# First block of a fused retention and two-FFN kernel: x split in two halves of 256 tokens, the first halves of two d_ff tiles between the attention chunks, weight conversion three steps ahead

## Chip, cores and metric

One NeuronCore of a Trainium2 chip runs the whole program in one launch. The metric is the device time of one execution in microseconds. Before the change three runs gave 883.71, 883.96 and 885.22 us: median 883.96 us.

## What is computed

A retention (linear attention with decay, no softmax) feeds an FFN with leaky ReLU, and that feeds an FFN with h·cos(h):

```python
def _attn_ref(q, k, v):                    # 4 batches, 8 heads, 576 tokens, 64 wide
    scores = scale * np.matmul(q, k.transpose(0, 1, 3, 2))
    Dmat = np.where(rel >= 0, gamma[:, None, None] ** rel[None, :, :], 0.0)
    return np.matmul(scores * Dmat[None], v)
x = attn_out.transpose(0, 2, 1, 3).reshape(2304, 512)
h = x @ w_in                               # d_ff = 2048
x = np.maximum(0.01 * h, h) @ w_out        # first FFN
h = x @ w_in2
out = (h * np.cos(h)) @ w_out2             # second FFN
```

## The kernel before

**Blocks and steps.** The 2304 tokens are five blocks (`TB`: 512, 512, 512, 384, 384). Each FFN runs over all blocks; a block goes through the 16 tiles f of 128 of d_ff, and one tile is a step s. `h_mm` (line 385) makes h of the step: 12 matmuls (4 parts of d_model, 3 products each) into one PSUM bank. `o_mm` (line 402) multiplies the tile of two steps earlier (`LAG`) with w_out, again 12 matmuls. So a step has 24 matmuls with up to 512 columns.

**Three products.** Operands of the FFN matmuls are float32r in two parts, high and low. `h_mm` issues for each part of d_model high weight by low x, low weight by high x, high by high: its first matmul needs the tile's high weight and the low x, its second the low weight. The x of a block is split by `split_x` (line 373): per part of d_model one copy on ACT (line 380: the high part) and one subtraction on DVE (line 381: the low part). After the first layer g is split the same way by `g_high` (ACT, line 455) and `g_low` (DVE, line 460).

**Weight conversion.** The raw weights arrive as 64-bit words. Each tile of the first FFN (a grain: 15 whole tiles, the last in two halves) is converted in five parts: `ready` calls `conv_a` (ACT, lines 307 and 308), `conv_b` (DVE, lines 313, 315, 319; a function `between` may be called ahead of line 319), `add_of` calls `conv_c` (DVE, line 326), `high_of` calls `conv_d` (ACT, line 335: the high weight), `low_of` calls `conv_e` (DVE, line 338: the low weight). Two buffers hold the grains under way, so `ready` of a grain needs the low part of the one two earlier.

**Retention.** It goes in chunks of 128 tokens: scale q and v by tables (line 135 on DVE for the first chunks), `scores` (line 166), `masks` (DVE, line 182), `values` (lines 197 and 211), `states` (DVE, lines 229 and 231: the running state), `reads` (line 244: the state's part), `take` (ACT, line 270: scaled output from PSUM to `xr`). Chunks 0 to 3 are the first block's x and run ahead of the steps; chunk 4 starts with `scores` after step 3 of the first block and follows the scaling of its q on DVE.

**What sets the order.** Under `manual_schedule` each engine runs its instructions in the order in which the code emits them. In the part ahead of the steps (lines 572 to 636) the four chunks, the conversion of grains 0 and 1 and the split of x are written out by hand:

```python
        conv_b(grains[1], second)          # line 619; second() is states(2)
        reads(2); take(2); states(3); reads(3); take(3)
        ...
        add_of(1); split_x(0); high_of(1); low_of(1); ready(2)
```

In the steps of the first block (lines 656 to 673) `conv_b` and `add_of` work on grain s + 2, `ready` on s + 3, and `low_of` on s + 1. The 16 matmuls of zeros at line 585 (`warm`) run on PE while the first data arrive.

Of the kernel before, what the change touches and what calls it, by code (L numbers as in the profile page):

```python
# [7 lines left out]
F32 = mybir.dt.float32  # L8
# [11 lines left out]
P = 128  # L20
# [48 lines left out]
def retention_ffn_ffn(  # L69
# [29 lines left out]
        tabs_sb[:, sum(sizes[:x]) : sum(sizes[: x + 1])] for x in range(4)  # L99
    )  # L100

    zero = xp.tile([P, 2 * T], F32, tag="x", name="zero")[:, :P]
    one = const.tile([P, 1], F32, name="one")
    psum = psp.tile([P, 8, 512], F32, name="psum")

# [83 lines left out]
    def values(i):  # L189
        b, ch, pt = banks_of(i), ch_t[i], p_t.pop(i)  # L190
        local = [(2 * i + x) % SUBS for x in range(2)]
        for p in range(NP):
            for x, tok in enumerate(halves):
                for e, r in enumerate(halves):
                    h = slice((2 * p + e) * D, (2 * p + e + 1) * D)
                    o = NP * C + p * C
                    nc.tensor.matmul(  # L197
                        psum[r, b + x, o : o + C],
                        ch[tok, 3, h],
                        pt[tok, e, p, :],  # L200
                        start=p == 0,
                        stop=local[x] == 0,
                        skip_group_check=True,
                    )
        for p in range(NP):
            for x, tok in enumerate(halves):
                if local[x] == SUBS - 1:
                    continue
                for e, r in enumerate(halves):
                    h = slice((2 * p + e) * D, (2 * p + e + 1) * D)  # L210
                    nc.tensor.matmul(  # L211
                        psum[r, b + x, p * D : (p + 1) * D],
                        ch[tok, 2, h],
                        ch[tok, 3, h],
                        start=False,
                        stop=True,
                        skip_group_check=True,
                    )
# [56 lines left out]
                )  # L275


    def warm(n, bank):
        for _ in range(n):
            nc.tensor.matmul(psum[:, bank, :P], zero, zero, start=True, stop=True)  # L280

# [26 lines left out]
    def conv_b(g, between=lambda: None):  # L310
        lo, hi = words(g)
        t = t_t[g]
        nc.vector.tensor_scalar(t, t, W_LO, W_HI, op0=ALU.max, op1=ALU.min)  # L313
        u = t.bitcast(U32)
        nc.vector.tensor_scalar(  # L315
            u, u, 3, 0x3FFFFFF8, op0=ALU.logical_shift_left, op1=ALU.bitwise_and
        )
        between()
        nc.vector.scalar_tensor_tensor(  # L319
            out=u, in0=hi, scalar=0xC0000000, in1=u, op0=ALU.bitwise_and, op1=ALU.bitwise_or  # L320
        )
# [49 lines left out]
            x_t[lj, k] = x  # L371
            nc.sync.dma_start(x[:, :, :n].bitcast(F32), x2[lj - NB][k])

    def split_x(lj):
        n = TB[lj]
        for k in range(KK):
            x = xp.tile([P, 2, T], F32R, tag="x", name="x_sb")
            x_t[lj, k] = x
            raw = xr.pop((lj, k))[:, :n]
            nc.scalar.copy(x[:, 0, :n], raw)  # L380
            nc.vector.tensor_tensor(  # L381
                out=x[:, 1, :n], in0=raw, in1=x[:, 0, :n].bitcast(F32), op=ALU.subtract
            )

    def h_mm(lj, f):
        l, n = lj // NB, TB[lj % NB]
        bank = BANK_H + (f % 2 if l == 0 else f % 4)
        hp = psum[:, bank, :n]
        h_t[lj, f] = hp
        wt, hi = w_t[l, f], l  # L390
        for k in range(KK):
            ks = slice(k * P, (k + 1) * P)
            for a, (i, j) in enumerate(((0, 1), (1, 0), (0, 0))):
                nc.tensor.matmul(  # L394
                    hp,
                    wt[:, i ^ hi, ks],
                    x_t[lj, k][:, j, :n],
                    start=(k == 0 and a == 0),
                    stop=(k == KK - 1 and a == 2),
                )  # L400
# [171 lines left out]
    with tc.manual_schedule():  # L572
        nc.scalar.dma_start(tabs_sb, tabs)
        nc.vector.memset(zero, 0.0)

        nc.scalar.copy(one, zero[:, :1])
        load_chunk(0)
        load_raw(0)
        for i in range(1, n_first):
            load_chunk(i)  # L580
        for f in range(1, 4):
            load_raw(f)
        scale_q(0)
        scale_v(0)
        warm(WARM[0], 3)
        scores(0)
        masks(0)
        ready(0)
        values(0)
        scale_v(1)  # L590
        conv_b(grains[0], lambda: scale_q(1))
        scores(1)
        masks(1)
        values(1)
        scale_v(2)
        states(0)
        reads(0)
        take(0)
        scale_q(2)
        scores(2)  # L600
        add_of(0)
        high_of(0)
        scale_q(3)
        scores(3)
        masks(2)
        ready(1)
        scale_v(3)
        values(2)
        low_of(0)
        masks(3)  # L610
        states(1)
        reads(1)
        take(1)
        values(3)

        def second():
            states(2)

        conv_b(grains[1], second)
        reads(2)  # L620
        take(2)
        states(3)
        reads(3)
        take(3)
        load_chunk(4)
        load_raw(4)
        load_chunk(5)
        for f in range(5, 10):
            load_raw(f)
        for _ in range(2):  # L630
            next_half()
        add_of(1)
        split_x(0)
        high_of(1)
        low_of(1)
        ready(2)

        for s in range(len(steps) + LAG[1]):
            lj, f = steps[s] if s < len(steps) else (None, None)
            i = chunk_at.get(s)  # L640
            if lj is not None:
                nxt = lj + 1 if lj + 1 < 2 * NB else None
                if s == last:
                    early.close()
                    fp = ctx.enter_context(tc.tile_pool(name="fp", bufs=2))
                if f == 2 and nxt is not None and nxt >= NB:
                    load_x(nxt)
                h_mm(lj, f)
                if f == NF - 1 and nxt is not None and nxt < NB:
                    split_x(nxt)  # L650
                if i is not None:
                    values(i)
                if s + 1 in chunk_at:
                    scores(chunk_at[s + 1])
            prev = steps[s - 1] if 1 <= s <= len(steps) else None
            if lj is not None and lj < NB:
                leaky(lj, f)
                if s < NF:

                    def between():  # L660
                        if s:
                            low_of(s + 1)
                        if s in (1, 2):
                            g_low(*prev)

                    if s + 2 < len(grains):
                        conv_b(grains[s + 2], between)
                    else:
                        between()
                    add_of(s + 2)  # L670
                    ready(s + 3)
                    high_of(s + 2)
                g_high(lj, f)
            if i is not None:
                states(i)
            if s + 1 in chunk_at:
                masks(chunk_at[s + 1])
            if n_first <= chunk_at.get(s + 2, 0) < n_busy:
                scale_q(chunk_at[s + 2])
                scale_v(chunk_at[s + 2])  # L680
            if prev and prev[0] < NB and prev in graw:
                g_low(*prev)
            for q in outs.get(s, ()):
                o_mm(*q)
            if i is not None:
                reads(i)
                take(i)
                if i + 2 < NCH:
                    load_chunk(i + 2)
                    if i + 2 >= n_busy:  # L690
                        scale_q(i + 2)
                        scale_v(i + 2)
            for q in outs.get(s, ()):
                if q[1] == NF - 1:
                    if lj is not None and lj < NB:

                        g_low(lj, f)
                    evacuate(q[0])
            if lj is not None and lj >= NB:
                cos_a(lj, f)  # L700
            if prev and prev[0] >= NB:
                cos_c(*prev)
            if lj is not None and lj >= NB:
                cos_b(lj, f)
            if prev and prev[0] >= NB:
                g_low(*prev)
            stash(s)
            for qj, qf in outs.get(s - 1, ()):
                if qj == NB - 1:
                    fetch_w(qf)  # L710
# [49 lines left out]
```

## Time and profile before

| what | value |
|---|---|
| median of three runs | 883.96 us |
| the profiled execution, its own time | 884.21 us |
| its span, first to last instruction | 882.4 us |
| PE busy | 862.1 us (98% of the span) |
| DVE busy | 577.0 us (65%) |
| ACT busy | 397.9 us (45%) |
| mean granted TensorE clock | 0.988 |

The profiled execution is 0.25 us above the median, and 1.8 us of its time lie outside the span. PE is the matmul engine, PEld its weight loads, DVE VectorE, ACT ScalarE, POOL GpSimd, SP the queue that issues most DMAs. A busy PE is not PE at its peak: matmuls overlap, and at the granted clock 0.50 they take about twice as long. Idle time of an engine costs only where PE or the chain that ends last waits for it.

### The profile page before, as it was taken

The page shows a single profiled execution, that of the slowest core. Times are in us where ns is not written, and L with a number is a line of the kernel's source. Part 1 is how long each engine was busy: PE and PEld are TensorE (multiplying, and loading weights), DVE is VectorE, ACT ScalarE, POOL GpSimd, SP SyncE. Part 2 cuts the span into 40 slices and gives each one's busy share as a digit, 9 for nine tenths or more (in the row PEclk, how much of TensorE's full clock was granted, in tenths as well). Part 3 has the DMA queues.
Part 4 walks back from the last instruction along what each step waited for, and adds up shares of the span by engine and source line. Part 5 has one row for each costly group of instructions (what it writes and reads, how often), then busy time and mean ns, then how long its engine had stood idle before and what let it go on. Part 6 is the DMA issues. An engine that isn't in the chain of part 4 may idle for free.

```text
span 882.4 us, 14824 instructions
## 1 busy us (share of the span) xinstructions
PE 862.1 (98%) x6048; PEld 752.6 (85%) x6048; DVE 577.0 (65%) x953; ACT 397.9 (45%) x738; POOL 69.0 (8%) x57
## 2 busy tenths in 40 slices
PE   6689999999999999999999999999999999999998
PEld 6568888778888888999999888888888888999998
DVE  5699964344644346644212897777777777888885
ACT  4588764434454446444322443343334333433433
POOL 0000020222212222211000000000000000000000
PEclk8699999999999999999999999999999999999999
DMA  9915421545464546641787700210021002100100
GB/s 362 418 48 196 184 100 72 192 168 175 161 238 144 192 147 247 218 155 49 284 305 245 262 1 1 95 49 1 1 72 48 1 1 72 49 1 1 37 1 36
DMA packets 35860, 110.88 MB, mean 126 GB/s; under 512 B 3408, under 2 KB 8528, under 8 KB 31696
## 3 DMA queue, kind: packets, MB, share of 16 engines
q1 hardware_dynamic: 35648, 109.59, 34.1%
q8 instruction: 47, 0.77, 0.4%
q10 hardware_dynamic: 144, 0.35, 0.1%
q14 instruction: 21, 0.17, 0.1%
HBM read 79.00 MB, written 30.93 MB: 125 GB/s over the span
## 4 chain that ended last, share of the span: by engine, by line
PE 94%; DVE 2%; DMA 1%; issue 1%; ACT 1%; SPq 0%; ACTq 0%
PE psum L408 45%; PE psum L394 44%; PE psum L244 2%; PE psum L166 1%; PE psum L197 1%; DMA raw<-in_w 1%; PE psum L211 1%; DVE t L326 1%; DVE t L319 1%; DVE w L338 0%; ACT t L307 0%; DVE g L460 0%; DVE t L313 0%; DVE t L315 0%; DVE p_sb L182 0%
## 5 line engine op out<-in xcount | busy, mean ns | idle before, releaser
L394 PE MATMUL psum<-x_sb,w 128*128 128x512 f32 (+1 forms) x1920 | 424.9, 370 | 4.2 <-DVE x_sb L381 2.5
L408 PE MATMUL psum<-g,w 128*128 128x512 f32 (+1 forms) x1920 | 424.1, 369 | 0.0
L394 PEld LDWEIGHTS psum<-x_sb,w 128*128 128x128 f32 x1920 | 351.0, 189 | 51.5 <-DVE x_sb L381 2.7
L408 PEld LDWEIGHTS psum<-g,w 128*128 128x128 f32 x1920 | 347.9, 188 | 46.7 <-DVE g L460 0.4
L455 ACT CAST g<-graw 128x512 fp32r<-128x512 f32 (+1 forms) x160 | 92.7, 579 | 238.3 <-PE psum L408 126.1
L460 DVE TENSOR_TENSOR g<-graw,g 128x512 fp32r<-128x512 f32 (+1 forms) x160 | 103.0, 645 | 92.1 <-ACT g L455 92.0
L478 ACT ACTIVATE r_sb<-r_sb 128x512 f32<-128x512 f32 (+1 forms) x80 | 47.3, 591 | 131.6 <-DVE r_sb L477 131.4
L468 DVE TENSOR_SCALAR t_sb<-psum 128x512 f32<-128x512 f32 (+1 forms) x80 | 51.0, 637 | 62.9 <-PE psum L394 62.9
L446 ACT ACTIVATE graw<-psum 128x512 f32<-128x512 f32 (+1 forms) x80 | 44.2, 553 | 57.9 <-PE psum L394 57.6
L476 DVE SCALAR_TENSOR_TENSOR r_sb<-t_sb,r_sb 128x512 f32<-128x512 f32 (+1 forms) x80 | 51.2, 640 | 2.8
L477 DVE SCALAR_TENSOR_TENSOR r_sb<-t_sb,r_sb 128x512 f32<-128x512 f32 (+1 forms) x80 | 51.1, 639 | 2.7
L475 DVE SCALAR_TENSOR_TENSOR r_sb<-t_sb,psum 128x512 f32<-128x512 f32 (+1 forms) x80 | 50.8, 635 | 2.8
L350 POOL TENSOR_TENSOR t<-t 128x512 fp32r<-128x512 f32 x32 | 42.6, 1338 | 126.9 <-ACT t L349 105.8
L484 DVE SCALAR_TENSOR_TENSOR graw<-r_sb,psum 128x512 f32<-128x512 f32 (+1 forms) x80 | 50.0, 625 | 1.7 <-ACT r_sb L479 1.7
L479 ACT ACTIVATE r_sb<-r_sb 128x512 f32<-128x512 f32 (+1 forms) x80 | 47.2, 590 | 2.5
L307 ACT ACTIVATE t<-raw 128x512 f32<-128x512 f32 (+1 forms) x49 | 39.9, 815 | 11.9 <-DMA raw<-in_w 8.0
L326 DVE CUSTOM_DVE_ANT_0 t<-raw,t 128x1024 uint16<-128x1024 uint16 (+1 forms) x49 | 41.9, 856 | 4.8
L319 DVE SCALAR_TENSOR_TENSOR t<-raw,t 128x512 uint32<-128x512 uint32 (+1 forms) x49 | 43.6, 891 | 1.1
L313 DVE TENSOR_SCALAR t<-t 128x512 f32<-128x512 f32 (+1 forms) x49 | 28.8, 587 | 18.7 <-ACT t L307 18.5
L182 DVE TENSOR_TENSOR p_sb<-psum,tabs_sb 128x512 f32<-128x512 f32 x18 | 12.4, 689 | 42.5 <-PE psum L166 40.9
L308 ACT ACTIVATE raw<-raw 128x512 int32<-128x512 uint32 (+1 forms) x49 | 39.8, 812 | 0.0
L473 DVE TENSOR_SCALAR t_sb<-t_sb 128x512 f32<-128x512 f32 (+1 forms) x80 | 31.6, 394 | 0.0
(35 smaller groups left out, 351.7 us busy)
## 6 DMA issues: line engine op xcount, KB each, us to landing
ch<-in_qkv SPq DMA_DIRECT2D x17, 1024.0 KB, 5.3
raw<-in_w SPq DMA_DIRECT2D x34, 512.0 KB, 4.2
w<-t SPq DMA_DIRECT2D x32, 512.0 KB, 3.0
w<-w SPq DMA_DIRECT2D x32, 512.0 KB, 5.2
raw<-in_w SPq DMA_DIRECT2D x15, 1024.0 KB, 8.7
x_sb<-x SPq DMA_DIRECT2D x12, 512.0 KB, 6.2
x<-x_hi SPq DMA_DIRECT2D x12, 256.0 KB, 2.5
x<-x_lo SPq DMA_DIRECT2D x12, 256.0 KB, 2.7
```

The costliest lines, as they stand in the source:

```text
L319: nc.vector.scalar_tensor_tensor(out=u, in0=hi, scalar=0xC0000000, in1=u, op0=ALU.bitwise_and, op1=ALU.bitwise_or)
L326: nc.vector.tensor_tensor(out=i, in0=i, in1=lo.bitcast(I32), op=ALU.add)
L394: nc.tensor.matmul(hp, wt[:, i ^ hi, ks], x_t[lj, k][:, j, :n], start=(k == 0 and a == 0), stop=(k == KK - 1 and a == 2),)
L408: nc.tensor.matmul(psum[:, BANK_O + m, :n], wt[:, i ^ hi, ms], gt[:, j, :n], start=(f == 0 and a == 0), stop=(f == NF - 1 and a == 2),)
L455: nc.scalar.copy(g_t[lj, f][:, 0, : TB[lj % NB]], g)
L460: nc.vector.tensor_tensor(out=gt[:, 1, :n], in0=graw.pop((lj, f)), in1=gt[:, 0, :n].bitcast(F32), op=ALU.subtract)
L468: nc.vector.tensor_scalar(t, h_t[lj, f], INV_2PI, MAGIC, op0=ALU.mult, op1=ALU.add)
L475: nc.vector.scalar_tensor_tensor(out=r, in0=t, scalar=-C1, in1=hp, op0=ALU.mult, op1=ALU.add)
L476: nc.vector.scalar_tensor_tensor(out=r, in0=t, scalar=-C2, in1=r, op0=ALU.mult, op1=ALU.add)
L477: nc.vector.scalar_tensor_tensor(out=r, in0=t, scalar=-C3, in1=r, op0=ALU.mult, op1=ALU.add)
L478: nc.scalar.activation(r, r, AF.Sin, scale=0.5)
L484: nc.vector.scalar_tensor_tensor(out=g, in0=sq_t.pop((lj, f)), scalar=0.5, in1=h_t.pop((lj, f)), op0=ALU.subtract, op1=ALU.mult,)
```

## The change

It does five things. The tile `zero` moves from the pool of x into a weight buffer that is free until grain 3, and gets 512 columns. Two matmuls of 512 columns of zeros stand on PE between `values(0)` and `scores(1)`. `split_x` and `h_mm` take a slice of tokens: the first block's x is split in tokens 0 to 255 after `take(1)`, and in tokens 256 to 511 after `take(3)`; tiles 0 and 1 take the first half ahead of `reads(2)` and `reads(3)`, and the second half at steps 0 and 1. Grain 2 is converted ahead of the steps as well. In the steps `conv_b` and `add_of` work on grain s + 3, `ready` on s + 4, `low_of` on s + 2, and `low_of` follows `g_low` inside `between`.

```diff
+        warm(2, 1, T)
         scale_v(1)
...
         values(3)
-        conv_b(grains[1], second)
+        split_x(0, slice(0, T // 2))
+        conv_b(grains[1], lambda: states(2))
+        ready(2)
+        h_mm(0, 0, slice(0, T // 2))
         reads(2)
+        add_of(1)
+        high_of(1)
         take(2)
-        states(3)
+        conv_b(grains[2], lambda: states(3))
+        low_of(1)
+        h_mm(0, 1, slice(0, T // 2))
         reads(3)
         take(3)
+        split_x(0, slice(T // 2, T))
+        add_of(2)
+        high_of(2)
...
-        add_of(1)
-        split_x(0)
-        high_of(1)
-        low_of(1)
-        ready(2)
+        ready(3)
...
-                h_mm(lj, f)
+                h_mm(lj, f, slice(T // 2, T) if s < 2 else None)
...
-                        if s:
-                            low_of(s + 1)
                         if s in (1, 2):
                             g_low(*prev)
+                        low_of(s + 2)
-                    if s + 2 < len(grains):
-                        conv_b(grains[s + 2], between)
+                    if s + 3 < len(grains):
+                        conv_b(grains[s + 3], between)
...
-                    add_of(s + 2)
-                    ready(s + 3)
-                    high_of(s + 2)
+                    add_of(s + 3)
+                    ready(s + 4)
+                    high_of(s + 3)
```

Three places of the order show it. **PE, from `reads(1)` to the third tile.** Before (w_338, w_538 and w_565 are the weights of tiles 0, 1 and 2):

```order
L244 MATMUL psum<-ch,st 64x64 x16
L197 MATMUL psum<-p_sb,ch 64x64 x16
L211 MATMUL psum<-ch 64x64 x16
L244 MATMUL psum<-ch,st 64x64 x32
L394 MATMUL psum<-x_sb,w_338 128x512 x12
L394 MATMUL psum<-x_sb,w_538 128x512 x12
```

Now (tiles 0, 1 and 2 are w_340, w_507 and w_562):

```order
L244 MATMUL psum<-ch,st 64x64 x16
L197 MATMUL psum<-p_sb,ch 64x64 x16
L211 MATMUL psum<-ch 64x64 x16
L394 MATMUL psum<-x_sb,w_340 128x256 x12
L244 MATMUL psum<-ch,st 64x64 x16
L394 MATMUL psum<-x_sb,w_507 128x256 x12
L244 MATMUL psum<-ch,st 64x64 x16
L394 MATMUL psum<-x_sb,w_340 128x256 x12
L394 MATMUL psum<-x_sb,w_507 128x256 x12
L394 MATMUL psum<-x_sb,w_562 128x512 x12
```

The 32 reads of chunks 2 and 3 have come apart, and each follows a half tile; the second halves come as two more runs of 12.

**DVE, from `states(1)` on.** Before (t_359, t_541 and t_562 are grains 1, 2 and 3):

```order
L231 TENSOR_TENSOR st<-psum,st 128x256 x2
L313 TENSOR_SCALAR t_359<-t_359 128x1024
L315 TENSOR_SCALAR t_359<-t_359 128x1024
L231 TENSOR_TENSOR st<-psum,st 128x256 x2
L319 SCALAR_TENSOR_TENSOR t_359<-raw,t_359 128x1024
L231 TENSOR_TENSOR st<-psum,st 128x256 x2
L326 ISA t_359<-raw,t_359 128x2048
L381 TENSOR_TENSOR x_sb<-xr,x_sb 128x512 x4
L338 TENSOR_TENSOR w_538<-t_359,w_538 128x1024
L313 TENSOR_SCALAR t_541<-t_541 128x1024
L315 TENSOR_SCALAR t_541<-t_541 128x1024
L319 SCALAR_TENSOR_TENSOR t_541<-raw,t_541 128x1024
```

Now, from the first half's split on, right behind the same `states(1)` (t_361 and t_475 are grains 1 and 2):

```order
L381 TENSOR_TENSOR x_sb<-xr,x_sb 128x256 x4
L313 TENSOR_SCALAR t_361<-t_361 128x1024
L315 TENSOR_SCALAR t_361<-t_361 128x1024
L231 TENSOR_TENSOR st<-psum,st 128x256 x2
L319 SCALAR_TENSOR_TENSOR t_361<-raw,t_361 128x1024
L326 ISA t_361<-raw,t_361 128x2048
L313 TENSOR_SCALAR t_475<-t_475 128x1024
L315 TENSOR_SCALAR t_475<-t_475 128x1024
L231 TENSOR_TENSOR st<-psum,st 128x256 x2
L319 SCALAR_TENSOR_TENSOR t_475<-raw,t_475 128x1024
L338 TENSOR_TENSOR w_507<-t_361,w_507 128x1024
L381 TENSOR_TENSOR x_sb<-xr,x_sb 128x256 x4
```

The split of x stood behind grain 1; now its first half stands ahead of grain 1, and the second half behind the low weight of tile 1 (w_507) and ahead of line 326 of grain 2.

**DVE, ahead of the scaling of chunk 4's q (line 135).** Before (t_589 and t_616 are grains 4 and 5, w_592 is tile 3):

```order
L313 TENSOR_SCALAR t_589<-t_589 128x1024
L315 TENSOR_SCALAR t_589<-t_589 128x1024
L338 TENSOR_TENSOR w_592<-t_562,w_592 128x1024
L460 TENSOR_TENSOR g<-graw,g 128x512
L319 SCALAR_TENSOR_TENSOR t_589<-raw,t_589 128x1024
L326 ISA t_589<-raw,t_589 128x2048
L135 TENSOR_TENSOR ch<-ch,tabs_sb 128x512
```

Now (t_606 is grain 4, t_633 grain 5, w_609 tile 3 and w_636 tile 4):

```order
L338 TENSOR_TENSOR w_609<-t_584,w_609 128x1024
L319 SCALAR_TENSOR_TENSOR t_606<-raw,t_606 128x1024
L326 ISA t_606<-raw,t_606 128x2048
L313 TENSOR_SCALAR t_633<-t_633 128x1024
L315 TENSOR_SCALAR t_633<-t_633 128x1024
L460 TENSOR_TENSOR g<-graw,g 128x512
L338 TENSOR_TENSOR w_636<-t_606,w_636 128x1024
L319 SCALAR_TENSOR_TENSOR t_633<-raw,t_633 128x1024
L326 ISA t_633<-raw,t_633 128x2048
L135 TENSOR_TENSOR ch<-ch,tabs_sb 128x512
```

The scaling stood behind line 326 of grain 4 and now stands behind that of grain 5, with the low weight of tile 4 ahead of it as well.

## Rows read from the trace of the kernel before

**Rows 1.** The page of the profiled execution: span, busy time by engine with its share of the span and the number of instructions, and the chain of waits that ended last, by engine.

```profile
span 882.4 us, 14824 instructions
...
PE 862.1 (98%) x6048; PEld 752.6 (85%) x6048; DVE 577.0 (65%) x953; ACT 397.9 (45%) x738; POOL 69.0 (8%) x57
...
PE 94%; DVE 2%; DMA 1%; issue 1%; ACT 1%; SPq 0%; ACTq 0%
```

**Rows 2.** Who PE (the matmul engine) waited for in the first 140 us: us in total, times, longest.

```profile
PE psum L394 <- DVE x_sb L381: 2.5, 1, 2.5
PE psum L211 <- issue: 2.2, 1, 2.2
...
PE psum L244 <- issue: 1.9, 1, 1.9
```

**Rows 3.** Groups of PE's instructions from 66.6 us to the end; the last column is the idle time before them.

```profile
L408 PE MATMUL psum<-g,w 128*128 128x512 f32 (+1 forms) x1884 | 415.2, 369 | 0.0
L394 PE MATMUL psum<-x_sb,w 128*128 128x512 f32 (+1 forms) x1860 | 407.7, 367 | 0.0
```

**Rows 4.** Busy time of DVE (VectorE) by stretch: us, the stretch's length, busy us and instructions, granted TensorE clock, DMA share, GB/s.

```profile
22.30:34.70 12.40, 6.22 (x12) 0.68 1.02 420
34.70:44.00 9.30, 8.81 (x11) 0.70 1.00 418
44.00:66.00 22.00, 21.39 (x25) 1.00 0.13 51
```

**Rows 5.** DVE in order of time: start us, us, line, operation, tiles, shape, count, and in brackets the idle time before it with what ended it.

```profile
22.37 0.88 DVE L231 TENSOR_TENSOR st<-psum,st 128x256 f32<-128x256 f32 x2
...
34.65 2.50 DVE L381 TENSOR_TENSOR x_sb<-xr,x_sb 128x512 fp32r<-128x512 f32 x4 [2.62 <-ACT x_sb L380]
37.15 1.23 DVE L338 TENSOR_TENSOR w<-t,w 128x1024 fp32r<-128x1024 f32 x1
...
42.40 0.69 DVE L313 TENSOR_SCALAR t<-t 128x1024 f32<-128x1024 f32 x1
...
48.51 0.69 DVE L313 TENSOR_SCALAR t<-t 128x1024 f32<-128x1024 f32 x1
...
49.84 1.22 DVE L338 TENSOR_TENSOR w<-t,w 128x1024 fp32r<-128x1024 f32 x1
50.98 0.69 DVE L460 TENSOR_TENSOR g<-graw,g 128x512 fp32r<-128x512 f32 x1
51.58 1.22 DVE L319 SCALAR_TENSOR_TENSOR t<-raw,t 128x1024 uint32<-128x1024 uint32 x1
...
53.98 0.69 DVE L135 TENSOR_TENSOR ch<-ch,tabs_sb 128x512 f32<-128x512 f32 x1
```

**Rows 6.** ACT (ScalarE) in order of time, same columns.

```profile
21.95 1.11 ACT L308 ACTIVATE raw<-raw 128x1024 int32<-128x1024 uint32 x1
26.00 1.14 ACT L270 ACTIVATE xr<-psum,tabs_sb 128x128 f32<-128x128 f32 x4 [2.94 <-PE psum L244]
...
33.98 2.19 ACT L380 CAST x_sb<-xr 128x512 fp32r<-128x512 f32 x4
...
41.23 1.13 ACT L307 ACTIVATE t<-raw 128x1024 f32<-128x1024 f32 x1
...
43.30 1.04 ACT L335 CAST w<-t 128x1024 fp32r<-128x1024 f32 x1
44.24 0.62 ACT L455 CAST g<-graw 128x512 fp32r<-128x512 f32 x1
```

**Rows 7.** PE in order of time, same columns.

```profile
1.05 6.29 PE L280 MATMUL psum<-zero 128*128 128x128 f32 x32 [1.05 <-DVE zero L574]
...
13.61 1.13 PE L166 MATMUL psum<-ch 64*64 64x64 f32 x32 [3.22 <-DVE ch L135]
...
30.95 1.97 PE L244 MATMUL psum<-ch,st 64*64 64x64 f32 x32 [0.52 <-DVE st L231]
35.39 8.07 PE L394 MATMUL psum<-x_sb,w 128*128 128x512 f32 x24 [2.47 <-DVE x_sb L381]
...
45.65 2.81 PE L394 MATMUL psum<-x_sb,w 128*128 128x512 f32 x11 [0.76 <-DVE w L338]
...
54.72 0.70 PE L166 MATMUL psum<-ch 64*64 64x64 f32 x32 [0.77 <-DVE ch L135]
...
65.97 0.68 PE L244 MATMUL psum<-ch,st 64*64 64x64 f32 x16 [0.81 <-DVE st L229]
```

**Rows 8.** Busy time of all engines by stretch: us, length, then busy us and instructions of PE, PEld (weight loads), DVE, ACT and POOL, granted clock, DMA share, GB/s. From 440 to 470 us the matmuls have 384 columns, from 510 to 550 us 512.

```profile
13.60:18.00 4.40, 3.49 (x108) 3.33 (x110) 4.25 (x6) 3.37 (x14) 0.00 (x0) 0.50 1.03 430
36.00:40.00 4.00, 4.00 (x11) 3.12 (x10) 3.93 (x6) 3.23 (x4) 0.00 (x0) 0.50 1.01 420
41.00:43.40 2.40, 2.40 (x11) 1.69 (x9) 2.19 (x3) 2.40 (x4) 0.00 (x0) 1.00 1.01 420
440.00:470.00 30.00, 30.00 (x175) 30.00 (x174) 3.91 (x7) 7.53 (x15) 0.00 (x0) 1.00 0.85 294
510.00:550.00 40.00, 40.00 (x178) 33.11 (x178) 33.45 (x56) 15.12 (x24) 0.00 (x0) 1.00 0.00 1
```

**Rows 9.** The weight loads of the first layer of an FFN (line 394): min, median and max ns.

```profile
L394 PEld LDWEIGHTS psum<-x_sb,w x1920: 186/188/338, 35.4 to 870.0; 128*128 128x128 f32 x192
```

**Rows 10.** DMA issues of the first 75 us: the loads of the raw weights, KB each and median us to landing.

```profile
raw<-in_w SPq DMA_DIRECT2D x12, 1024.0 KB, 10.1
```

More of the change, by code (lines that the diff above doesn't have):

```diff
@@ L100, in retention_ffn_ffn @@
     )
-    zero = xp.tile([P, 2 * T], F32, tag="x", name="zero")[:, :P]
+    zero = wp.tile([P, T], F32, tag=f"w{NF // 4 - 1}", name="zero")
     one = const.tile([P, 1], F32, name="one")
@@ L275, in take, with warm @@
                 )
-    def warm(n, bank):
+    def warm(n, bank, cols=P):
         for _ in range(n):
-            nc.tensor.matmul(psum[:, bank, :P], zero, zero, start=True, stop=True)
+            nc.tensor.matmul(psum[:, bank, :cols], zero[:, :P], zero[:, :cols], start=True, stop=True)
     w_t, raw_t, t_t, rawp_t = {}, {}, {}, {}
@@ L372, in load_x, with split_x, h_mm @@
             nc.sync.dma_start(x[:, :, :n].bitcast(F32), x2[lj - NB][k])
-    def split_x(lj):
-        n = TB[lj]
+    def split_x(lj, at=None):
+        at = at or slice(0, TB[lj])
         for k in range(KK):
[L377 to L380, printed above, removed]
+            if at.start == 0:
+                x_t[lj, k] = xp.tile([P, 2, T], F32R, tag="x", name="x_sb")
+            x, raw = x_t[lj, k], xr[lj, k][:, at]
+            nc.scalar.copy(x[:, 0, at], raw)
             nc.vector.tensor_tensor(
-                out=x[:, 1, :n], in0=raw, in1=x[:, 0, :n].bitcast(F32), op=ALU.subtract
+                out=x[:, 1, at], in0=raw, in1=x[:, 0, at].bitcast(F32), op=ALU.subtract
             )
-    def h_mm(lj, f):
+    def h_mm(lj, f, at=None):
         l, n = lj // NB, TB[lj % NB]
         bank = BANK_H + (f % 2 if l == 0 else f % 4)
-        hp = psum[:, bank, :n]
-        h_t[lj, f] = hp
+        h_t[lj, f] = psum[:, bank, :n]
+        at = at or slice(0, n)
         wt, hi = w_t[l, f], l
@@ L394, in h_mm @@
                 nc.tensor.matmul(
-                    hp,
+                    psum[:, bank, at],
                     wt[:, i ^ hi, ks],
-                    x_t[lj, k][:, j, :n],
+                    x_t[lj, k][:, j, at],
                     start=(k == 0 and a == 0),
@@ L614, in retention_ffn_ffn @@
         values(3)
-        def second():
-            states(2)
-        conv_b(grains[1], second)
+        split_x(0, slice(0, T // 2))
+        conv_b(grains[1], lambda: states(2))
+        ready(2)
+        h_mm(0, 0, slice(0, T // 2))
         reads(2)
+        add_of(1)
+        high_of(1)
         take(2)
-        states(3)
+        conv_b(grains[2], lambda: states(3))
+        low_of(1)
+        h_mm(0, 1, slice(0, T // 2))
         reads(3)
         take(3)
+        split_x(0, slice(T // 2, T))
+        add_of(2)
+        high_of(2)
         load_chunk(4)
```

## The prediction

> **What bounds the kernel now.** I read the page first: PE is busy for 862.1 of 882.4 us and makes up 94% of the chain that ended last [rows 1]. From 66.6 us to the end its two large groups wait for nothing [rows 3]. So whatever the change does to the time, it does in the first 66 us, and lateness of PE there is not made up later: a PE with no idle time has nothing to give back.
>
> Next, who PE waited for in the first stretch: 2.5 us for the low x before the first tile, and two waits of 2.2 and 1.9 us for "issue", in which the profile shows nothing that it waits for [rows 2]. In order of time: tile 0 starts at 35.39, tile 2 gets its low weight at 45.65, `scores` of chunk 4 comes at 54.72 after 0.77 us for line 135 on DVE, and the last wait, 0.81 us, ends at 65.97 [rows 7].
>
> Then the stretches of DVE: from 22.3 to 34.7 us it is busy for 6.22 of 12.40 us, then for 8.81 of 9.30 and 21.39 of 22.00 us [rows 4]. Before 34.7 us it has 6.2 us to spare; behind that DVE feeds PE and has nothing to spare. The change has to be judged on DVE: does it fill those 6.2 us, and what comes ahead of what PE waits for?
>
> **The granted clock.** It was 0.50 from 13.6 to 18 us after PE's wait of 3.22 us, and 0.50 from 36 to 40 us, after the wait of 2.47 us that followed scattered small matmuls; from 41 us on 1.00 [rows 7, 8]. 0.50 is 1.2 GHz, 1.00 is 2.4 GHz. Tiles 0 and 1 took 8.07 us for 24 matmuls that cost 24 x 40.00/178 = 5.4 us at full clock: such a restart cost 2.7 us.
>
> **The edits that cost nothing.** `zero` in another buffer, and its larger memset (0.7 us at most, as any 512 columns on DVE [rows 5]), stand ahead of the data's arrival. The two zero matmuls fill PE's wait of 3.22 us before `scores(1)`: the 16 of 128 columns at the start took 6.29 us [rows 7], so by columns two of 512 take 3.1 us, less if PE is at full clock by then. If that cover were gone they would cost those 3.1 us. What they may give is a full clock for chunks 1 and 2; I take that into the start below. The raw loads that reuse the buffers of chunks 2 and 3 go out later on SP, those behind them too; a load of 1024 KB lands after 10.1 us [rows 10], and the first of these grains is converted tens of us later: nothing.
>
> **The new chain, step by step.** Prices are start-to-start differences of neighbouring rows where the engine is full.
>
> 1. *Start.* `take(1)` needs `reads(1)`. It cannot start before ACT has finished `ready(1)`, 21.95 + 1.11 = 23.06 us, and before it started at 26.00 [rows 6]. With faster small matmuls, but the same waits for "issue", I take 24.8, between the two.
> 2. *First half's split.* `take` lasts 1.14, four casts of 512 columns 2.19 [rows 6]; the first of 256 ends about 0.4 after `take`. Four subtractions of 512 columns took 2.50 [rows 5]; at the 0.42 of a 256-column DVE instruction (22.37 row: 0.88 for two [rows 5]) 1.5. DVE: 26.2 to 27.7. From `states(1)` (over at 23.25 before, perhaps 22.7 now) to 26.2 DVE has nothing to do: line 381 heads its queue and the conversion of grain 1 stands behind it.
> 3. *Grains 1 and 2 on DVE.* Lines 313 and 315 take 1.33 (48.51 to 49.84), line 338 1.14 (to 50.98), lines 319 and 326 2.40 (51.58 to 53.98) [rows 5], two state additions 0.8, line 319 alone about 1.2. 27.6 + 1.33 + 0.8 + 2.40 + 1.33 + 0.8 + 1.15 = 35.4, then line 338 gives tile 1 its low weight at 36.7. Before that was 37.15 + 1.23 = 38.4 [rows 5].
> 4. *The wait that the change adds.* Next on DVE is the second half's split. Its x comes from `take(3)`, that from `reads(3)`, and PE runs `reads(3)` behind the first half of tile 1, which needs the low weight made a moment ago. So from 36.7: 11 matmuls of 256 columns; 32 reads; `take(3)` 1.14; a cast. The matmul price: 440 to 470 us gives 30.00/175 = 0.171 us for 384 columns, 510 to 550 us 0.225 for 512 [rows 8]; by the same slope 0.118 for 256, at half clock twice that. PE has waited since about 30 us but for one matmul, so I take 0.50: 2.6 us. The reads: 1.97 at 0.50, and twice the 0.68 of 16 at full clock [rows 7]. With the pipeline's tail line 381 runs at 36.7 + 2.6 + 0.2 + 1.95 + 1.4 = 42.85. **DVE stands still for 6.1 us.**
> 5. *Behind it.* Split 1.5, line 326 of grain 2 until 45.45; then ACT casts its high weight (1.04) before it may start `ready(3)`, whose first part takes 1.13 [rows 6], since `high_of(2)` stands ahead of `ready(3)`. Line 313 of grain 3 starts at 47.6, where before it started at 42.40 [rows 5]: 5.2 us late.
> 6. *One more grain ahead of chunk 4.* From here DVE runs without a gap that PE could cause. Before, line 135 followed 11.6 us after that line 313 (42.40 to 53.98 [rows 5]). Now grains 3, 4 and 5 stand ahead of it: 1.33 + 1.14 + 2.40 for grain 3 with the low weight of tile 2, then twice 1.33 + 0.60 for g + 1.14 + 2.40, and about 0.4 each in which g waits for its high part on ACT (a cast of 1.04 and one of 0.62 [rows 6] against 1.33 on DVE): 16.6 us. 47.6 + 16.6 = 64.2, and `scores(4)` 0.74 later, as before, at 64.95, against 54.72: **10.2 us late**. PE has then been through tile 3 (by about 61 us) and waits.
> 7. *After that.* The same work in the same order. The wait of 0.81 at 65.97 [rows 7] should go, as PE is later against DVE. The wait ahead of `scores(4)`, some 4 us, is longer than those that were followed by 0.50, so up to one restart of 2.7 us; I take half, 1.35.
>
> Sum: 10.2 - 0.8 + 1.35 = 10.75 us. 884.2 + 10.75 = 894.95 for the profiled execution; the median of the runs lies 0.25 lower: **894.7 us**.
>
> **Two rules of the Trainium skill against the rows.** PE's two waits for "issue" add up to 4.1 us [rows 2]. The page Runtime: NRT & Kernel Launch (Instruction fetch mechanics) says that fetching the next block of instructions is mostly hidden; if "issue" were no more than that and hidden here, `take(1)` would start at 23.06 and the sum would be 1.7 us less, 893.0; these rows speak against it.
>
> A weight load lasts 188 ns [rows 9], more than the 118 ns I give a matmul of 256 columns. TensorE: Matmul & The Clock Gate (LDWEIGHTS) puts a load at columns over 1.2, by which 128 columns are 107 ns and would not set the pace. The rows don't settle it: 384 columns already go at 171 ns with loads of 188, so loads overlap, but no row has 256. If 188 were a floor (338 at half clock [rows 9]) step 4 would be 1.1 us longer, 895.8.
>
> **Bounds.** Low: `take(1)` at 23.06 (-1.7), clock 1.00 for tile 1 and the reads (-1.3, -0.6) and after `scores(4)`: 10.2 - 3.6 - 0.8 = +5.8, 889.8. High: `take(1)` at 26.00 (+1.2), loads as the floor (+1.1), a full restart and no wait saved: 10.2 + 2.3 + 2.7 = +15.2, 899.2.
>
> **The rivals.**
> - *The clock holds.* The zero matmuls and half tiles keep PE at 1.00 throughout: 10.2 - 1.9 - 0.8 = +7.5, **891.4 us**. For it: less time between bursts. Against it: step 4's wait for line 338 is there at any clock. Chance 0.22.
> - *Half clock up to some 70 us*, with loads setting the pace: **898 us**. Chance 0.15.
> - *Lateness is absorbed*, the grain ahead paying for it: **884 us**. It needs idle time of PE later on, and there is only the 0.81 us. Chance 0.03.
> - *Faster: DVE's idle time is really filled.* If x of each half were there when line 381 reaches the head of DVE's queue, DVE would save its 6.2 us before 34.7 and do 4.87 us more for the extra grain and 0.5 for smaller pieces ahead of line 135: at best 1 us earlier at `scores(4)`, 0.8 at 65.97: **882 us**. It decides at one point: the second half's x must be on ACT's output at 36.7, 6 us before I see it. Step 4 hangs on the low weight of tile 1, which DVE makes last, so I give it 0.03.
>
> **The numbers.** Forecast as summed: 0.57. Below it the clock that holds, above it the half clock; 890.0 to 899.0 takes in nearly all of the bounds and leaves out the two cases without a loss. A measurement of this kernel can tell about 0.2% (1.8 us) from no change: faster 0.03, same 0.03, slower 0.94.
>
> **What would show it.** DVE idle for about 6 us before the second line 381, PE's `scores(4)` near 65 us after a wait of some 4 us for line 135, no wait of PE behind 70 us. Wrong, if line 313 of grain 3 starts before 43 us, or if PE's wait for line 135 is under 1 us.

## The result: 1.3% slower

Four runs of the changed kernel gave 893.94, 894.93, 895.61 and 895.93 us, median **895.27 us**; four of the kernel before in the same series have the median 883.97. The ratio is 1.013 (95% interval 1.0117 to 1.0142). Predicted were 894.7 us and a range of 890.0 to 899.0.

The profiled execution took 893.94 us, the lowest of the four; that of before took 884.21. The two profiles differ by 9.73 us, the medians by 11.3. What the other three runs have on top of the profiled one no trace shows, so the steps below are held against the 9.73 us.

### The profile page after: what moved, and what is told of

The parts are those of the page before. It is cut to its first block, busy times and chain, and to the rows that moved or that the text cites. A ratio compares the mean times of both kernels' runs of the same rounds, so it can differ in the third digit from the quotient of the medians.

```text
span 892.1 us, 14883 instructions
## 1 busy us (share of the span) xinstructions
PE 865.4 (97%) x6076; PEld 754.4 (85%) x6076; DVE 576.9 (65%) x957; ACT 398.6 (45%) x742; POOL 68.9 (8%) x57
## 4 chain that ended last, share of the span: by engine, by line
PE 92%; DVE 0%; issue 0%; ACT 0%
PE psum L408 45%; PE psum L394 43%; PE psum L244 2%; PE psum L166 1%; PE psum L197 1%; PE psum L211 1%; DVE t L326 0%; DVE w L338 0%; DVE t L319 0%; DVE ch L135 0%; ACT o_sb L423 0%; DVE g L460 0%
## 5 line engine op out<-in xcount | busy, mean ns | idle before, releaser
L394 PE MATMUL psum<-x_sb,w 128*128 128x512 f32 (+2 forms) x1944 | 428.0, 369 | 10.8 <-DVE w L338 3.6
```

The source lines that it names most:

```text
L394: nc.tensor.matmul(psum[:, bank, at], wt[:, i ^ hi, ks], x_t[lj, k][:, j, at], start=(k == 0 and a == 0), stop=(k == KK - 1 and a == 2),)
```

## The profile after

The page (columns as in [rows 1]):

```profile
span 892.1 us, 14883 instructions
...
PE 865.4 (97%) x6076; PEld 754.4 (85%) x6076; DVE 576.9 (65%) x957; ACT 398.6 (45%) x742; POOL 68.9 (8%) x57
```

PE works 3.3 us longer than before, and the span is 9.7 us longer: two thirds of what was lost is waiting. Who PE waited for in the first 140 us (us in total, times, longest), beside [rows 2]:

```profile
PE psum L166 <- DVE ch L135: 6.4, 4, 4.3
PE psum L394 <- DVE w L338: 3.6, 2, 3.0
PE psum L394 <- DVE x_sb L381: 3.1, 2, 2.0
PE psum L394 <- ACT w L335: 2.3, 1, 2.3
...
PE psum L211 <- issue: 1.1, 1, 1.1
...
PE psum L394 <- issue: 0.7, 1, 0.7
```

The waits for "issue" have shrunk from 4.1 to 1.8 us. In their place PE waits for DVE: 4.3 us once for line 135, 3.0 once for the low weight of line 338, 2.0 for the second half of x. From 76.3 us to the end its groups are as idle-free as in [rows 3]:

```profile
L408 PE MATMUL psum<-g,w 128*128 128x512 f32 (+1 forms) x1884 | 415.2, 369 | 0.0
L394 PE MATMUL psum<-x_sb,w 128*128 128x512 f32 (+1 forms) x1860 | 407.7, 367 | 0.0
```

The same counts and the same busy time: all of the loss lies ahead of this point. DVE in order of time, beside [rows 5] (start, us; in brackets the idle time before and who ended it):

```profile
21.93 0.87 DVE L231 TENSOR_TENSOR st<-psum,st 128x256 f32<-128x256 f32 x2
25.52 1.43 DVE L381 TENSOR_TENSOR x_sb<-xr,x_sb 128x256 fp32r<-128x256 f32 x4 [2.72 <-ACT x_sb L380]
...
34.77 1.22 DVE L338 TENSOR_TENSOR w<-t,w 128x1024 fp32r<-128x1024 f32 x1
41.83 1.43 DVE L381 TENSOR_TENSOR x_sb<-xr,x_sb 128x256 fp32r<-128x256 f32 x4 [5.84 <-ACT x_sb L380]
43.17 1.22 DVE L326 CUSTOM_DVE_ANT_0 t<-raw,t 128x2048 uint16<-128x2048 uint16 x1
46.55 0.69 DVE L313 TENSOR_SCALAR t<-t 128x1024 f32<-128x1024 f32 x1 [2.16 <-ACT t L307]
...
63.23 0.68 DVE L135 TENSOR_TENSOR ch<-ch,tabs_sb 128x512 f32<-128x512 f32 x1
```

Three times DVE stands still: 2.72 us for the first half of x, 5.84 for the second, 2.16 for ACT's first part of grain 3. Then it runs almost without a gap to line 135, which comes at 63.23 where it came at 53.98. ACT, which feeds it, beside [rows 6]:

```profile
24.05 1.15 ACT L270 ACTIVATE xr<-psum,tabs_sb 128x128 f32<-128x128 f32 x4 [0.74 <-PE psum L244]
...
40.36 1.14 ACT L270 ACTIVATE xr<-psum,tabs_sb 128x128 f32<-128x128 f32 x4 [6.70 <-PE psum L244]
41.38 1.33 ACT L380 CAST x_sb<-xr 128x256 fp32r<-128x256 f32 x4
44.43 1.04 ACT L335 CAST w<-t 128x1024 fp32r<-128x1024 f32 x1 [1.72 <-DVE t L326]
45.38 1.14 ACT L307 ACTIVATE t<-raw 128x1024 f32<-128x1024 f32 x1
```

The row at 40.36 is `take(3)`: ACT itself has waited 6.70 us for PE's `reads(3)`. And PE, beside [rows 7]:

```profile
26.00 1.22 PE L394 MATMUL psum<-x_sb,w 128*128 128x256 f32 x8 [1.06 <-DVE x_sb L381]
...
36.04 2.72 PE L394 MATMUL psum<-x_sb,w 128*128 128x256 f32 x11 [3.00 <-DVE w L338]
38.69 1.62 PE L244 MATMUL psum<-ch,st 64*64 64x64 f32 x32
42.31 4.63 PE L394 MATMUL psum<-x_sb,w 128*128 128x256 f32 x24 [2.00 <-DVE x_sb L381]
...
63.97 1.13 PE L166 MATMUL psum<-ch 64*64 64x64 f32 x32 [4.28 <-DVE ch L135]
65.03 3.96 PE L408 MATMUL psum<-g,w 128*128 128x512 f32 x12
...
76.31 3.02 PE L394 MATMUL psum<-x_sb,w 128*128 128x512 f32 x12
```

Read in a ring, the last three fences show one of the two losses that the experiments below tell apart: PE waits for DVE's low weight (36.04), `reads(3)` stands behind that half tile (38.69), ACT waits for the reads (40.36), DVE waits for ACT (41.83). DVE stood still for 5.84 us because of a weight that it made itself just before. PE's granted clock (stretch, length, busy us and instructions, clock, DMA share, GB/s):

```profile
33.50:39.50 6.00, 3.46 (x26) 0.50 0.52 217
43.30:46.40 3.10, 3.10 (x16) 0.50 1.00 420
50.00:53.20 3.20, 3.20 (x9) 0.50 0.78 270
54.00:63.50 9.50, 5.69 (x24) 1.00 0.01 3
63.80:66.90 3.10, 2.93 (x36) 0.50 0.00 0
67.20:76.00 8.80, 8.80 (x90) 1.00 0.38 125
```

The clock is at 0.50 (1.2 GHz) in four of these stretches, the last behind the wait of 4.28 us, and at 1.00 from 67.2 on.

## The experiments

Theory: two losses that add up. One is the ring just shown, the other the deeper lead, which puts a whole grain more of DVE's work ahead of line 135. The halves as such, with their 24 more matmuls, cost nothing. The numbers in brackets are the ratio to the kernel before and its 95% interval. Times are medians; the kernel before had 883.49 us in the series of the first four kernels, 883.74 in that of the next four, 883.89 in that of the last two. Amounts in us are differences of ratios times 884.

**Open the ring, keep the rest.** `reads(3)` and `take(3)` go ahead of the first half of tile 1:

```diff
-        h_mm(0, 1, slice(0, T // 2))
         reads(3)
         take(3)
+        h_mm(0, 1, slice(0, T // 2))
```

> Undoes the added wait alone: reads(3) and take(3) stand ahead of the first half of tile 1, so they no longer wait for that tile's low weight. Theory (two separate losses on DVE: about 4 us for the second half's split that waits for take(3), about 5 us for one more grain ahead of chunk 4): DVE waits under 2 us before the second split instead of 5.8, line 313 of grain 3 starts near 42.5 us instead of 46.6, but line 135 of chunk 4 stays about 16.6 us behind it, near 59 us, and PE still waits for it: 891 us, about 4 less than the changed kernel. Rival 'the deeper lead alone': 895, no change. Rival 'half tiles on PE and its clock': 895, since the matmuls are the same. Rival 'the wait alone': 884 to 885.

Measured: **891.66 us**, ratio 1.0092 (1.0079 to 1.0104). DVE:

```profile
26.38 1.43 DVE L381 TENSOR_TENSOR x_sb<-xr,x_sb 128x256 fp32r<-128x256 f32 x4 [3.18 <-ACT x_sb L380]
...
38.14 1.43 DVE L381 TENSOR_TENSOR x_sb<-xr,x_sb 128x256 fp32r<-128x256 f32 x4 [1.28 <-ACT x_sb L380]
...
42.84 0.69 DVE L313 TENSOR_SCALAR t<-t 128x1024 f32<-128x1024 f32 x1 [2.14 <-ACT t L307]
...
59.53 0.69 DVE L135 TENSOR_TENSOR ch<-ch,tabs_sb 128x512 f32<-128x512 f32 x1
```

The second split waits 1.28 instead of 5.84 us, and everything behind it comes 3.7 us earlier, line 135 too. It still lies 16.7 us behind line 313 of grain 3, and PE still waits 4.22 us for it:

```profile
60.27 1.13 PE L166 MATMUL psum<-ch 64*64 64x64 f32 x32 [4.22 <-DVE ch L135]
61.33 5.35 PE L408 MATMUL psum<-g,w 128*128 128x512 f32 x12
```

The ring is worth 3.4 us (1.0130 - 1.0092); what is left is another cause. Between the two profiled runs it is 2.3 us (893.94 - 891.66): `scores(4)` comes 3.70 us earlier, but the twelve matmuls behind it take 5.35 us here and took 3.96 in the changed kernel, 1.4 us more.

**Take back the lead, keep the ring.** Grain 2 is converted in step 0 again, the halves stay:

```diff
-        conv_b(grains[2], lambda: states(3))
+        states(3)
...
-        add_of(2)
-        high_of(2)
...
-        ready(3)
...
-                        low_of(s + 2)
...
-                    add_of(s + 3)
-                    ready(s + 4)
-                    high_of(s + 3)
+                    add_of(s + 2)
+                    ready(s + 3)
+                    high_of(s + 2)
```

`conv_b` works on grain s + 2 and `low_of` on s + 1 again, as before.

> Undoes the deeper lead alone: grain 2 is converted in step 0 again and the steps work on grain s + 2; the halves and the order of reads stay as changed. Theory: the low weight of tile 1 comes about 2 us earlier, DVE still waits 5 to 6 us before the second split, line 313 of grain 3 starts near 45, line 135 only 11 to 11.5 us later, near 56.5, scores of chunk 4 near 57 to 59: 887 us (886 to 888). Rival 'the wait alone': 893 to 895. Rival 'half tiles on PE and its clock': 895. Rival 'the deeper lead alone': 884.

Measured: **887.21 us**, 1.0041 (1.0029 to 1.0053). DVE:

```profile
40.45 1.43 DVE L381 TENSOR_TENSOR x_sb<-xr,x_sb 128x256 fp32r<-128x256 f32 x4 [6.18 <-ACT x_sb L380]
...
45.66 0.68 DVE L313 TENSOR_SCALAR t<-t 128x1024 f32<-128x1024 f32 x1
...
56.58 0.68 DVE L135 TENSOR_TENSOR ch<-ch,tabs_sb 128x512 f32<-128x512 f32 x1
```

The ring is there in full, 6.18 us. But from grain 3 to line 135 it is now 10.9 us instead of 16.7, and `scores(4)` starts without a wait, as soon as PE is through with tile 3:

```profile
58.06 0.69 PE L166 MATMUL psum<-ch 64*64 64x64 f32 x32
```

The lead is worth 7.9 us (1.0130 - 1.0041).

**Both edits together.**

> Undoes both: halves and the two zero matmuls stay, reads(3) ahead of the first half of tile 1, lead of two. Theory (the two losses add up and nothing else costs): about as before the change, 883 us (882 to 884), DVE waits 2 us or less before the second split, line 135 of chunk 4 near 52.5. Rival 'half tiles on PE and its clock': 24 more matmuls of 256 columns and what they do to the clock are still here, so 890 or more.

Measured: **882.97 us** in 12 runs, 0.9996 (0.9988 to 1.0005): as before the change. DVE:

```profile
35.92 1.43 DVE L381 TENSOR_TENSOR x_sb<-xr,x_sb 128x256 fp32r<-128x256 f32 x4 [1.24 <-ACT x_sb L380]
...
52.43 0.69 DVE L135 TENSOR_TENSOR ch<-ch,tabs_sb 128x512 f32<-128x512 f32 x1
```

In sum the half tiles between the chunks, the 24 more matmuls and the zero matmuls are free; what each of them gives or takes by itself this run does not tell. The two losses add up: the ring 4.0 us here (1.0041 - 0.9996), the lead 8.5 (1.0092 - 0.9996), 11.8 together.

**The lead alone**, x whole, neither halves nor zero matmuls between `values(0)` and `scores(1)` (against the changed kernel; in the steps `h_mm` takes the whole block again):

```diff
-        h_mm(0, 0, slice(0, T // 2))
-        h_mm(0, 1, slice(0, T // 2))
-        split_x(0, slice(0, T // 2))
-        split_x(0, slice(T // 2, T))
-        add_of(2)
-        high_of(2)
-        warm(2, 1, T)
...
+        split_x(0)
+        add_of(2)
+        high_of(2)
         ready(3)
```

> The kernel before with the deeper lead alone: x is split whole after take(3), no halves, no second group of zero matmuls, grain 2 converted ahead of the steps, the steps work on grain s + 3. Theory: line 313 of grain 3 starts near 41, a little earlier than before the change (42.4), but line 135 of chunk 4 comes 16.6 us later instead of 11.6, near 57.5, and PE waits 4 to 5 us for it: 888.5 us (888 to 889). Rival 'half tiles on PE and its clock' or 'the wait alone': 884 or less, since the conversion runs ahead in idle time.

Measured: **887.93 us**, 1.0054 (1.0041 to 1.0067), just under the range expected. PE's waits from 45 to 140 us:

```profile
PE psum L166 <- DVE ch L135: 2.6, 1, 2.6
PE psum L408 <- DVE g L460: 2.0, 1, 2.0
```

I had expected one wait of 4 to 5 us for line 135; it is two, 2.0 us for g and 2.6 for line 135, on the same DVE. Alone, the lead costs 4.8 us, with the halves and the ring open 8.1; the difference is 3.4 us (1.0092 - 1.0054). Between the profiled runs it is 3.9 us: 2.7 are there at `scores(4)` (57.58 against 60.27), the rest is half clock behind it. DVE shows where the 2.7 come from. Here it goes from `states(1)` straight into grain 1, at 23.07; in the kernel with the ring open it stands still for 3.18 us ahead of the first split, and grain 1 starts at 27.73. With the lead of three DVE has work for the time before x; the first split at the head of its queue keeps it from it. No run took that one wait away by itself, so this share is read from the two traces, not tried.

**Is it line 135's place?** The kernel of the last run, with q of chunk 4 scaled ahead of the steps, where line 135 has nothing in front of it:

```diff
+        scale_q(n_first)
...
-                scale_q(chunk_at[s + 2])
+                if chunk_at[s + 2] > n_first:
+                    scale_q(chunk_at[s + 2])
```

> The deeper lead alone, as in the run with x split whole, and the scaling of chunk 4's q (line 135) moved from behind grain 5 to ahead of the steps, on DVE behind line 326 of grain 2. Theory (all of DVE's queue stands one grain too far back for chunk 4, not this one instruction): PE no longer waits for line 135, but from 2 to 5 us each time for what stands next on DVE, g_low of step 2 and the masks of chunk 4, so the time falls by about 1 us only, 887 us (886.3 to 887.5) against 887.9. Rival 'line 135 is what costs': about 4 us less, 884.

Measured: **887.06 us**, 1.0034 (1.0022 to 1.0047). Line 135 is over by 39.3 us (38.66 + 0.68) and `scores(4)` starts without a wait at 54.02, but

```profile
48.31 3.06 PE L408 MATMUL psum<-g,w 128*128 128x512 f32 x12 [2.03 <-DVE g L460]
...
63.26 0.69 PE L197 MATMUL psum<-p_sb,ch 64*64 64x64 f32 x32 [2.88 <-DVE p_sb L182]
```

PE waits as long for the masks (line 182), the next thing of chunk 4 that DVE makes. The lead costs because DVE has a grain more to do before chunk 4, wherever line 135 stands.

**The zero matmuls.** The changed kernel without `warm(2, 1, T)`:

> The changed kernel without the two matmuls of 512 columns of zeros ahead of scores(1). Theory: they cost nothing and save a restart of the clock in chunks 1 and 2, so without them take(1) and all that hangs on it come about 1 us later: 896.5 us (895.5 to 898). Rival 'the zero matmuls delay scores(1)': 892 to 894.

Measured: **896.22 us** (893.88 to 896.83), 1.0135 (1.0121 to 1.015). The range overlaps that of the changed kernel, so the times don't tell whether these matmuls help here. In the two traces `take(1)` comes at 25.54 without and at 24.05 with them; but over the traces of all the kernels here it comes between 24.05 and 25.22 with them and between 24.41 and 26.12 without, so this is not clear either.

**Towards a faster version.** What does bound the start of the kernel before? In its trace DVE's state addition at 29.93 has waited 2.37 us for PE's matmuls with the state, and three buffers hold the state in turn:

```profile
29.93 0.97 DVE L231 TENSOR_TENSOR st<-psum,st 128x256 f32<-128x256 f32 x2 [2.37 <-PE psum L244]
```

The kernel before, with the last states of the first chunks in weight buffers that are still free:

```diff
-            new = ap.tile([P, NP * D], F32, tag="st", name="st", bufs=3)
+            home = {5: f"w{NF // 2 - 1}", 6: f"w{NF // 2 - 2}", 7: "w2"}.get(2 * i + x + 1)
+            if home:
+                new = wp.tile([P, NP * D], F32, tag=home, name="st")
+            else:
+                new = ap.tile([P, NP * D], F32, tag="st", name="st", bufs=3)
```

> The kernel before with one edit: states 5, 6 and 7 (of chunks 2 and 3) get homes of their own in weight buffers that are free until later, instead of the three buffers that rotate. Theory: in the kernel before DVE's idle time ahead of 34.7 us comes from state additions that wait for the reads of an earlier state to free its buffer (up to 2.4 us), so with them gone the split of x starts near 33 us and what follows on DVE comes 1 to 2 us earlier, and the restart of the clock may go too: 880.5 us (879.5 to 882.5). Rival 'the split waits for take(3) anyway': 883 to 884.

Measured: **881.85 us**, 0.9979 (0.997 to 0.9988), as expected. That addition (now line 235: in this kernel and the next, lines behind the edit have numbers that are 4 higher) starts earlier and hardly waits:

```profile
26.85 0.95 DVE L235 TENSOR_TENSOR st<-psum,st 128x256 f32<-128x256 f32 x2 [0.19 <-PE psum L211]
```

The same with the zero matmuls of the change:

> The kernel before with the three homes for states 5, 6 and 7 and the two zero matmuls of the change ahead of scores(1); no halves, lead of two. Theory: full clock through chunks 1 and 2 adds about 1 us: 879.5 us (878.5 to 881). Rival 'the zero matmuls do nothing': as with the states alone.

Measured: **882.02 us**, 0.9978 (0.9969 to 0.9988): a miss, they give nothing. Tiles 0 and 1 without and with them:

```profile
33.21 7.32 PE L398 MATMUL psum<-x_sb,w 128*128 128x512 f32 x24 [2.57 <-DVE x_sb L385]
```

```profile
33.99 8.35 PE L398 MATMUL psum<-x_sb,w 128*128 128x512 f32 x24 [2.47 <-DVE x_sb L385]
```

From 13.6 to 18 us the granted clock is 0.74 with them and 0.50 without. That gain is gone before it is needed: from 34 to 37 us, in tiles 0 and 1, it is 0.50 with them and 0.57 without.

**Loads later.** The kernel before, with the raw load of grain 3 issued behind `take(3)`, and on SP all later loads behind it; so that it waits for `reads(2)`, grain 3 takes the buffer of chunk 2 (`ROOM`):

```diff
-    ROOM = (13, 12, 11, 10, 9, 8, 15, 14, 13, 12, 15, 14, 13, 15, 14)
+    ROOM = (13, 12, 11, 15, 9, 8, 10, 14, 13, 12, 15, 14, 13, 15, 14)
...
-        for f in range(1, 4):
+        for f in range(1, 3):
...
+        load_raw(3)
```

> The kernel before with the raw loads from grain 3 on (and those of chunks 4 and 5, which stand behind them on SP) held back: grain 3 takes the buffer of chunk 2, so its load and all behind it start only after reads(2), near 31 us; the DMA engines have nothing of the program to move from about 24 to 31 us. Theory on PE's waits for 'issue' (blocks of PE's own instructions that come by DMA and queue behind the loads): the second one, 1.9 us near 29.5, is gone or under 0.7 us, the first, near 23.3, is at most a little shorter; the split of x comes 1 to 2 us earlier: 882.7 us (881.5 to 884). Rival 'issue has nothing to do with DMA': both waits stay, 884.

Measured: **880.42 us**, 0.9961 (0.9948 to 0.9975): faster, and by more than expected. PE from 23 to 31 us, in this kernel and in the kernel before:

```profile
23.00:31.00 8.00, 5.68 (x160) 0.79 0.28 95
```

```profile
23.00:31.00 8.00, 5.22 (x150) 0.73 1.01 420
```

The DMA engines are busy for 0.28 of this stretch instead of all of it, the second wait for "issue" is gone, and x is split at 31.00 instead of 34.65. DVE:

```profile
27.11 0.95 DVE L231 TENSOR_TENSOR st<-psum,st 128x256 f32<-128x256 f32 x2 [0.70 <-PE psum L244]
...
31.00 2.50 DVE L381 TENSOR_TENSOR x_sb<-xr,x_sb 128x512 fp32r<-128x512 f32 x4 [1.80 <-ACT x_sb L380]
```

The state addition that waited 2.37 us waits 0.70 here, with its three buffers as they were. So most of that wait was PE's wait for "issue" in the reads ahead of it. Both edits together:

> The same held-back loads on top of the homes for states 5 to 7. Theory: the second wait for 'issue' (1.8 us) is gone, take(3) and the split of x come up to 2 us earlier (line 381 near 31 us instead of 32.5): 880.3 us (879.3 to 881.5) against 881.9 for the states alone. Rival: 881.9.

Measured: **879.61 us** (879.38 to 881.01), 0.9957 (0.9944 to 0.9969): as expected, the lowest median of all and faster than both kernels, though it can't be told apart from the one with the later loads alone. Alone the two edits give 1.9 and 3.4 us, together 3.8: they take away largely the same wait.

## Why the prediction was right, step by step

- **Start (1, 2).** `take(1)` at 24.05 against 24.8 predicted, the first split at 25.52 against 26.2: 0.7 us early, and nearly all the steps behind carry that along. The kernels of the first three experiments are the same up to here, and their `take(1)` comes at 24.91, 24.45 and 24.86: 24.8 was a fair guess, and the 0.7 us lie within the spread between executions.
- **Low weight of tile 1 (3).** Line 338 ends at 35.99, predicted 36.7.
- **The added wait (4).** The step on which all rested. DVE stood still for 5.84 us (6.1 predicted), the second split came at 41.83 (42.85). The 11 matmuls of 256 columns took 2.65 us to the first read (2.6 predicted; by their starts in the trace they come 0.213 us apart, where the prediction had 0.236, and the first took longer); the reads 1.62 (1.95), since the clock rose on the way.
- **Grain 3 (5).** Line 313 at 46.55 against 47.6, after 2.16 us for ACT's line 307, which came behind the cast of line 335 as foreseen.
- **The extra grain (6).** From there to line 135 16.68 us, predicted 16.6; `scores(4)` at 63.97 after 4.28 us (64.95, some 4). It is 9.25 us late against 54.72, where 10.2 were predicted: the 0.7 of the start and 0.3 of the reads.
- **After that (7).** Predicted +0.55; it is +0.48 (9.73 - 9.25). `scores(4)` and the twelve matmuls behind it took 1.13 and 3.96 us against 0.70 and 3.06 before [rows 7], 1.3 us for half a restart, and the wait of 0.81 is gone. That it was the half is luck: behind a wait of 4.22 us the same rows took 1.13 and 5.35 us in the run with the ring open, 2.7 us, the whole restart.

The sum for the profiled execution was 894.95 and it took 893.94. That the median of 895.27 lies so near the predicted 894.7 is partly chance: I expected it 0.25 below the profiled run, and it lies 1.3 above. A longer half clock behind `scores(4)` in the other three runs would fit that (their mean granted clock is 0.987, 0.987 and 0.982 against 0.989), but is not shown.

The rivals: the clock did not hold (0.50 in four stretches; the one in tile 2, from 50.0 to 53.2 us, cost nothing in the end, as PE stood still for line 135 behind it), nor did it stay low to 70 us, a rival whose 898 us the prediction gave without a sum. Nothing was absorbed, as the idle-free groups say. And the point on which "faster" hung failed as foreseen: the second half's x was ready at 41.83, not at 36.7.

Of the two rules weighed, the first (Runtime: NRT & Kernel Launch, Instruction fetch mechanics, of the Trainium skill) would have had `take(1)` at 23.06; it came at 24.05, after 1.1 us of "issue", so what stands behind this wait was not hidden. By the second (LDWEIGHTS in TensorE: Matmul & The Clock Gate, of the Trainium skill) loads would not set the pace, and so it is: with loads as the floor, the other price that the prediction gave, eleven matmuls would have taken 3.7 us, and they took 2.65. Its figure of 107 ns does not hold for these loads: they last 188 ns at full clock [rows 9] and 328 at half clock.

One point the prediction did not separate. Its steps 5 and 6 give 5.2 us to the wait and 5.0 to the grain; taken back singly they are worth 3.4 to 4.0 and 7.9 to 8.5. With the lead taken back and the ring kept, line 135 comes 6.65 us earlier (56.58). PE gets 5.91 of these, as `scores(4)` then stands behind tile 3 (58.06 against 63.97), and the half clock behind PE's long wait, 1.3 us, is gone too: 7.2 us, against 7.1 between the two profiled runs (893.94 - 886.85). So the restart of step 7 belongs to the lead, and so does 0.9 us of the lateness of grain 3 (line 313 at 45.66 against 46.55): lines 313, 315 and 319 of grain 2 stand ahead of the low weight of tile 1.

## What to carry to other kernels

Before work is put ahead on an engine that runs in order, ask for each instruction at the head of its queue whether what it waits for hangs on something that the same engine makes just before: here DVE, PE, ACT and DVE made a ring of 5.84 us. Idle time of an engine early on is only worth filling if the work behind it that another engine awaits comes no later; a lead that is one grain deeper put 5.8 us of DVE's work ahead of the next consumer, with no slack on PE to take it up. And if a consumer's wait only changes its name when one instruction is moved (line 135, then line 182), it is the amount of work, not its place.

## What the runs showed of the hardware that was not expected

- **Weight loads overlap each other and the matmuls.** From 43.3 to 46.4 us PE was busy throughout with matmuls of 256 columns at the granted clock 0.50, and by their starts in the trace they come 0.213 us apart. The weight loads of this stretch (count, busy us, mean ns):

```profile
L394 PEld LDWEIGHTS psum<-x_sb,w 128*128 128x128 f32 x16 | 3.5, 328 | 0.0
```

One after another, 16 loads of 0.328 us would take 5.2 us; together they took 3.5. The page TensorE: Matmul & The Clock Gate (The mechanism) of the Trainium skill has a sentence by which a load overlaps a matmul only in another row group, and one by which a load into the background weight buffer is pulled ahead as well. These matmuls use all rows, so the first does not hold here; the second would fit, but no run shows which buffer a load goes to.
- **Waits for "issue" end when a block of instructions has come by DMA, and with busy DMA engines that block comes later.** The page of the profile has a DMA queue "instruction" (q8), and the trace has its blocks of 16 KB with their times. Each of the waits of PE for "issue" between 20 and 30 us, in all of these kernels, begins after the same number of PE's matmuls and weight loads, 705 or 961, and ends 1.2 to 1.5 us after such a block has landed. In the kernel before, the second of these blocks was moved from 27.14 to 28.24 us, 3.8 us after the first wait, and PE went on at 29.55; with the loads held back it was moved from 23.51 to 24.92, 1.1 us after that wait, and PE, which gets that far near 26.8, did not stop. When a block was asked for no record shows. Five kernels without half tiles whose loads went on at full rate through the stretch from 24 to 31 us show the second wait, 1.8 to 2.9 us; the two in which the loads came later (DMA share 0.28 from 23 to 31 us in the first) don't. With half tiles the second wait is 0.7 or 1.5 us, or absent, at the full DMA share. The first wait, 1.1 to 2.4 us, is there in every kernel.
- **A full clock gained early is not kept.** Zero matmuls at 11 us raised the clock from 13.6 to 18 us, it was 0.50 again in tiles 0 and 1, and the time in a kernel without half tiles stayed (0.9978 with them, 0.9979 without).
